# Linear attention and two gated feed-forward layers in one launch: free order of the products, new planner costs and due times, and k^T v in column halves

## Chip, cores and metric

The kernel runs on one NeuronCore of one Trainium2 chip, as one launch. The metric is the device time in microseconds of an execution. Times before and after come from several runs; one more execution of the kernel was taken with the hardware profiler, and all rows below come from it.

## What is computed

q, k and v have the shape (4, 8, 576, 64): batches, heads, tokens, width. The matrices of the two feed-forward layers have 512 x 1536 and 1536 x 512 elements and reach the kernel as 64-bit floats; q, k and v as 32-bit floats.

```python
q_s = softmax(q, axis=-1); k_s = softmax(k, axis=2)      # sums + 1e-9
kv = einsum('bhsd,bhse->bhde', k_s, v)
x = einsum('bhsd,bhde->bhse', q_s, kv)                   # -> (2304 tokens, 512)
x = (silu(x @ w_gate) * (x @ w_val)) @ w_out             # layer 0
out = ((x @ w_a) * (x @ w_b)) @ w_out2                   # layer 1
```

## The kernel before

**Stages.** The attention is done in 16 units, one for each batch b (4) and pair of heads g (4), by `attend` (L528 to L811). Each unit turns the maximum of k over the tokens (L669, L674), subtracts it and takes the exponential (L706, L710), multiplies k^T v on TensorE (L732, L733: four tiles of 128 tokens and one of the 64 last tokens of both heads), scales the two 64 x 64 blocks on the diagonal (L744, L748), normalises and turns q (L767 or L771, L780, L783) and multiplies it by the scaled blocks (L793, L803). For b = 0 q is taken less its row maximum on GpSimd (L698, L702), one ACT instruction of 1280 elements takes the exponentials of k and q (L706), a DVE reduction sums the rows (L756) and GpSimd multiplies by the reciprocals (L767). For b > 0 each row group has an exponential of its own on ACT, with the maximum as bias and the sum as a second output (L717), and GpSimd normalises (L771, L774).

The feed-forward layers work in fp32: each operand is split into two fp32r parts (high and low), and each product is three matmuls of 512 columns (high x low, low x high, high x high). A cast on ACT makes the high part (L333 or L438), and a subtraction on DVE or GpSimd makes the low one (L326). The 12 column tiles f of layer 0's matrices (`w0_0` to `w0_11`) are loaded and converted from 64 bits by `convert` (L359 to L443): absolute value (ACT L412 or DVE L414), scaling of the low word (ACT L417), clamp (DVE L419), shift (DVE L422), sign (DVE L428), the sum of the words (DVE or GpSimd L433), then the split. The activations of token block 0, `xhl0_0`, come straight from the units of b = 0.

Layer 0 runs over the blocks i = 0 and 1 (512 tokens each) tile by tile: `up` (L859, `ups` L844 for the first tile) makes the two products u of tile f, `gated` makes silu(u0) x u1 and splits it (`h`), and `down` (L886) adds the output product of the tile before, `acc`. The other stretches, layer 0's blocks 2 and 3 with the 256 last tokens, and layer 1, are three super-steps of six steps each (`step`, L1056 onwards): products p of sums and differences of blocks (L1138, seven where plain blocks would take eight), q of the last tokens (L1222), and output products o (L1248, L1250, L1257), which DVE adds into `sums` (`plus`, L1143).

**What sets the order.** `Plan` (L33 to L241) records every operation with an engine, a cost, its dependences, sometimes a second engine that may take it, and a due time, and then simulates the engines: at each moment the ready operation that is due first is issued on its engine, and this order is the program's order. `prepare` works the due times out backwards from the products' own, which `product` (L828) sets: the sum of the costs so far. `product` also adds an order edge to the product before, so all products of the feed-forward layers stand on TensorE in the order in which the code makes them, and only the attention's matmuls slip between them. `search` (L217) tries 160 sets of due times, each with some 3% of them moved by up to 3 us at random, and keeps the one with the shortest planned length.

TensorE, DVE, ACT and GpSimd each work their list strictly in that order; loads and stores stand on SP's queue, a few on ACT's.

Of the kernel before, what the change touches and what calls it, by code (L numbers as in the profile page):

```python
# [31 lines left out]
class Plan:  # L32
# [58 lines left out]
    def hop(self, first, then, other):  # L91

        if first != then:
            return other
        return 0.0 if first == "tensor" else self.SAME

    def prepare(self):
# [7 lines left out]
        for n in reversed(range(len(ops))):  # L105
# [4 lines left out]
            for s in self.succ[n]:  # L110
                if n in ops[s]["hold"]:
                    continue
                hop = self.hop(op["engine"], ops[s]["engine"], self.SLACK) + lands if n in ops[s]["deps"] else 0.0
                t = min(t, self.due[s] - hop)
# [5 lines left out]
    def order(self):  # L120
# [37 lines left out]
        while len(done) < len(ops):  # L158
# [25 lines left out]
            if port:  # L184
                port_free = t + cost
# [8 lines left out]
            free[engine] = t + cost  # L194
# [13 lines left out]
            for s in succ[n]:  # L208
                left[s] -= 1
                if not left[s]:  # L210
                    at = ops[s]["engine"]
                    is_ready(s, max([end[d] + self.hop(ops[d]["runs"][run[d]][0], at, self.HOP)
# [4 lines left out]
    def search(self):  # L217

        self.prepare()
        rng, best = random.Random(0), None  # L220
        for n in range(self.ROUNDS):
            kept = self.due
            if best:
                self.due = [d + rng.uniform(-3, 3) if rng.random() < 0.03 else d for d in kept]
            try:
                found = self.order()
            except RuntimeError:
                self.due = kept
                continue
            if best and self.length > best[0]:  # L230
                self.due = kept
            else:
                best = self.length, found
        return best[1]

    def emit(self):
        done, run, slot = self.search()
# [7 lines left out]
def kernel(  # L245
# [90 lines left out]
    def dma(fn, nbytes, reads, writes, due=None, after=(), issue=0.475, queue="sync", hold=()):  # L336
# [5 lines left out]
    def load(fn, nbytes, writes, issue=0.475):  # L342
# [4 lines left out]

    mats = [[m.bitcast(U32) for m in ms] for ms in ((w_gate, w_val, w_out), (w_a, w_b, w_out2))]
# [4 lines left out]
    TOP = 122880.0  # L353
    LEAST = 2.0 ** -15
# [102 lines left out]
    def convert_late(f, m):  # L457
# [23 lines left out]
        dma(get, P * 2 * WH * 8, [], [LOW, HIGH], issue=0.95 if m < 2 else 0.475, after=first)  # L481
# [46 lines left out]
    def attend(b, g, xhl, due):  # L528
# [63 lines left out]
        def qraw():  # L592
            return col(Q, q0, n)
# [781 lines left out]
```

## Time and profile before

| | us |
|---|---|
| median of 3 runs | 942.72 (940.71 to 944.29) |
| the profiled execution | 941.4 |
| its span, from the first to the last instruction | 939.2 |
| TensorE (PE) busy | 904.6, 4400 matmul passes |
| weight loads (PEld) busy | 753.0, beside the matmuls |
| VectorE (DVE) busy | 638.1 |
| ScalarE (ACT) busy | 518.3 |
| GpSimd (POOL) busy | 334.9 |
| mean granted TensorE clock | 0.996 of 2.4 GHz |

An engine that is busy for nearly the whole span sets the time; what another engine does counts only where the first one waits for it. A 32-bit matmul is recorded as two passes, an fp32r matmul as one. "Idle before" is the time in which an engine had nothing running before an instruction, and the name behind the arrow is what ended it.

### The profile page before, as it was taken

Reading aid. Unit: us, or ns where it says so; the run is one execution under the profiler, and the core shown is the slowest. Engines: PE = TensorE matmul, PEld = TensorE weight load, DVE = VectorE, ACT = ScalarE, POOL = GpSimd, SP = SyncE. Lnnn points to the kernel's source line nnn. Section 1 sums busy time; section 2 is a strip of 40 time slices with the busy share of each in tenths; the row PEclk is TensorE's granted clock in tenths of the full one; section 3 lists DMA queues with packets and bytes.
Section 4 is the critical chain, followed back from the end, with each engine's and each line's share of the span. In section 5 each row is a group of like instructions: output and inputs, shape, how many; then the busy total and the mean of one; then the engine's idle time right before and its main releaser. Section 6 shows DMA issues by size and latency. Waiting matters only on the chain.

```text
span 939.2 us, 12787 instructions
## 1 busy us (share of the span) xinstructions
PE 904.6 (96%) x4400; PEld 753.0 (80%) x4400; DVE 638.1 (68%) x1025; ACT 518.3 (55%) x1020; POOL 334.9 (36%) x323
## 2 busy tenths in 40 slices
PE   5599999999999999999999999999999999999998
PEld 3477777788887888888888888888888888888886
DVE  6999996544376887877778665875796444564444
ACT  4798876878675665455464546443644453333310
POOL 6534221212052322435555633442565113242210
PEclk9989999999999999999999999999999999999999
DMA  9858765464327555354322753422223210110003
GB/s 271 273 204 263 237 224 192 122 195 131 88 90 234 157 147 156 120 165 154 112 91 72 228 183 101 135 89 90 68 66 115 79 46 22 45 46 23 23 1 112
DMA packets 108153, 121.42 MB, mean 129 GB/s; under 512 B 31929, under 2 KB 83897, under 8 KB 107961
## 3 DMA queue, kind: packets, MB, share of 16 engines
q1 hardware_dynamic: 102424, 116.55, 39.7%
q10 hardware_dynamic: 5664, 4.07, 1.4%
q8 instruction: 34, 0.56, 0.2%
q14 instruction: 31, 0.25, 0.1%
HBM read 88.60 MB, written 31.98 MB: 128 GB/s over the span
## 4 chain that ended last, share of the span: by engine, by line
PE 83%; DVE 5%; ACT 4%; DMA 3%; issue 2%; SPq 1%; POOL 1%; ACTq 0%; DVEq 0%; POOLq 0%
PE p L1138 35%; PE o L1248 15%; PE u L859 10%; PE q L1222 7%; PE o L1250 6%; PE acc L886 5%; PE o L1257 2%; DMA wr<-in_moe_w_out_dram 1%; PE xt L793 1%; DVE l2w L326 1%; ACT ut L717 1%; ACT a L412 1%; PE kv L732 1%; SPq L620 1%; DMA wf<-latewr 1%
## 5 line engine op out<-in xcount | busy, mean ns | idle before, releaser
L1138 PE MATMUL p<-l2w,l2w 128*128 128x512 f32 x1512 | 352.8, 389 | 1.2 <-DVE temps L326 1.2
L1138 PEld LDWEIGHTS p<-l2w,l2w 128*128 128x128 f32 x1512 | 283.1, 188 | 61.2 <-DVE temps L326 2.5
L859 PE MATMUL u<-xhl,w 128*128 128x512 f32 x552 | 143.3, 407 | 5.0 <-DVE w L326 4.8
L326 POOL TENSOR_TENSOR l2w<-raww,l2w 128x512 fp32r<-128x512 f32 x68 | 97.2, 1434 | 94.1 <-ACT l2w L333 94.0
L333 ACT CAST l2w<-raww 128x512 fp32r<-128x512 f32 x144 | 87.9, 621 | 74.9 <-PE p L1138 39.7
L859 PEld LDWEIGHTS u<-xhl,w 128*128 128x128 f32 x552 | 101.9, 191 | 31.8 <-DVE w L326 7.1
L326 DVE TENSOR_TENSOR sums<-o,sums 128x512 f32<-128x512 f32 x120 | 82.3, 689 | 53.2 <-PE o L1248 39.4
L326 DVE TENSOR_TENSOR temps<-p,temps 128x512 f32<-128x512 f32 x90 | 62.1, 690 | 67.1 <-PE p L1138 65.9
L1248 PE MATMUL o<-l2w,hp 128*128 128x512 f32 x288 | 97.0, 391 | 0.6 <-DVE sums L326 0.6
L1150 ACT COPY temps<-p 128x512 f32<-128x512 f32 x72 | 42.4, 588 | 67.3 <-PE p L1138 67.1
L326 DVE TENSOR_TENSOR l2w<-raww,l2w 128x512 fp32r<-128x512 f32 x76 | 57.1, 762 | 26.5 <-ACT l2w L333 26.3
L886 PE MATMUL acc<-h,w 128*128 128x512 f32 x288 | 72.1, 395 | 0.0
L1222 PE MATMUL q<-rest,l2w 128*128 128x256 f32 x432 | 65.4, 283 | 0.0
L1248 PE MATMUL o<-l2w 128*128 128x512 f32 x192 | 64.4, 389 | 0.0
L1248 PEld LDWEIGHTS o<-l2w,hp 128*128 128x128 f32 x288 | 53.4, 188 | 12.6 <-DVE sums L326 1.9
L886 PEld LDWEIGHTS acc<-h,w 128*128 128x128 f32 x288 | 52.9, 188 | 10.6
L1222 PEld LDWEIGHTS q<-rest,l2w 128*128 128x128 f32 x432 | 58.6, 192 | 0.9
L1250 PE MATMUL o<-hp,l2w 128*128 128x512 f32 x144 | 48.6, 391 | 1.4 <-DVE sums L326 1.4
L1248 PE MATMUL o<-l2w,l2w 128*128 128x512 f32 x168 | 49.6, 389 | 0.0
L1250 PE MATMUL o<-l2w 128*128 128x512 f32 x144 | 48.3, 389 | 0.0
L498 POOL TENSOR_TENSOR latewr<-latewr 128x512 uint32<-128x512 uint32 x17 | 24.0, 1413 | 61.5 <-DVE latewr L493 52.7
L326 POOL TENSOR_TENSOR raww<-raww,spare 128x512 f32<-128x512 f32 x15 | 20.1, 1341 | 68.7 <-DVE l2w L326 63.2
(197 smaller groups left out, 1470.9 us busy)
## 6 DMA issues: line engine op xcount, KB each, us to landing
raww<-wf SPq DMA_DIRECT2D x36, 512.0 KB, 4.3
raww<-wf SPq DMA_DIRECT2D x36, 256.0 KB, 3.4
wf<-latewr SPq DMA_DIRECT2D x36, 256.0 KB, 3.2
wf<-a SPq DMA_DIRECT2D x16, 384.0 KB, 2.7
latewr<-in_moe_w_a_dram SPq DMA_DIRECT2D x24, 256.0 KB, 2.9
latewr<-in_moe_w_b_dram SPq DMA_DIRECT2D x24, 256.0 KB, 3.7
latewr<-in_moe_w_out_dram SPq DMA_DIRECT2D x12, 512.0 KB, 5.0
wr<-in_moe_w_gate_dram SPq DMA_DIRECT2D x22, 256.0 KB, 2.9
```

What stands on the lines that cost most here:

```text
L326: engine.tensor_tensor(out=out(), in0=x(), in1=y(), op=op)
L333: add("scalar", act_us(n), lambda: nc.scalar.copy(out=hi(), in_=src()), src_keys, [hi_key])
L412: add("scalar", act_us(e) + 0.08, lambda rows=rows, halves=halves: nc.scalar.activation(out=a(halves).bitcast(F32), in_=rows()[..., 1].bit ...
L498: engine.tensor_tensor(out=u32(), in0=u32(), in1=r()[..., 0], op=ALU.add)
L859: nc.tensor.matmul(ps()[:, 0:n], lhsT=wv[:, c, :], rhs=x()[:, xs, c, 0:n], start=(a == 0 and c == 0), stop=(a == 2 and c == KD - 1))
L886: nc.tensor.matmul(ps()[:, 0:n], lhsT=w()[:, 4 + ws, o * P:(o + 1) * P], rhs=h()[:, hs, 0:n], start=begin, stop=end)
L1138: nc.tensor.matmul(ps()[:, 0:width], lhsT=wv(o)[:, m, ws, c, :], rhs=ops_x[o][xs][1]().rearrange("p (c n) -> p c n", c=2)[:, c, 0:width], ...
L1150: add("scalar", act_us(n), lambda: nc.scalar.copy(out=to[1]()[:, 0:n], in_=ps()[:, 0:n]), [ps], [to[0]], due=main["at"] + main["soon"])
L1222: nc.tensor.matmul(ps[m]()[:, 0:256], lhsT=wv(o)[:, m, ws, c % 2, :], rhs=rest_x[xs][1]().rearrange("p (c n) -> p c n", c=KD)[:, c, :], st ...
L1248: nc.tensor.matmul(ps(), lhsT=lhs(i, hs), rhs=outs_w[i][1]()[:, ws * 512:(ws + 1) * 512], **ends)
L1250: nc.tensor.matmul(ps()[:, 0:width], lhsT=outs_w[i][1]()[:, ws * 512 + r * P:ws * 512 + (r + 1) * P], rhs=hs2[i][t][1]()[:, hs * 512:hs * ...
L1257: nc.tensor.matmul(ps()[:, o * 256:(o + 1) * 256], lhsT=outs_w[i][1]()[:, ws * 512 + at:ws * 512 + at + P], rhs=rest_h[1]()[:, (2 * i + hs ...
```

## The change

Five things are edited. `product` no longer ties a product to the one before, so the planner may issue any product whose operands are there. The planner's constants for hops between engines, DMA and issue costs are new, with new terms for the overlap of consecutive instructions of an engine (`OVER`) and of the port that DVE and GpSimd share (`PORT`); some operations have new costs. The random search is gone: the due times of 332 operations are moved by the amounts of a table, `MOVES`, and the order is made once. The units 1 and 3 of b = 0 (`BYROW`) take q's exponentials row by row on ACT as the later batches do, and for b = 0's other two units ACT may normalise q in place of GpSimd (ten `scalar.mul` of 64 columns). k^T v is computed in column halves: for each of the five token tiles two matmuls, one for each head, with 64 columns of weights and 65 moving columns (64 of v and the ones), written to the lower and upper half of the partitions; before, it was one matmul with 128 columns of weights and 130 moving ones, half of whose result was not used. `FLAT` and `NORM` are empty and change nothing.

```diff
-    SAME, HOP = 0.1, 0.17
+    SAME, HOP, TO_TENSOR, TO_GPSIMD, FROM_TENSOR = 0.033, 0.06, 0.055, 0.1, 0.2
+    OVER = dict(vector=0.08, scalar=0.115, gpsimd=0.045)
+    PORT = 0.08
-    DMA_START, DMA_END, DMA_RATE, DMA_LANES = 1.1, 1.5, 290e3, 8
-    TABLE = 1.3
+    DMA_START, DMA_END, DMA_RATE, DMA_LANES = 1.0, 1.35, 393e3, 8
+    TABLE = 1.43
-    ROUNDS = 160
+    MOVES = (
+        6, 46.2, 8, 113.4, 9, 15.3, 27, 8.1, 35, 6.2, 38, -3.9, 41, -42.6, 51, 1.8, 55, -14.4, 60, -15.5,
...
+    )
...
-                port_free = t + cost
+                port_free = t + cost - self.PORT
...
-            free[engine] = t + cost
+            free[engine] = t + cost - self.OVER.get(engine, 0.0)
...
-    def search(self):
...
+    def emit(self):
         self.prepare()
...
+        for n, us in zip(self.MOVES[::2], self.MOVES[1::2]):
+            self.due[n] += us
+        done, run, slot = self.order()
...
+    NORM = ()
+    BYROW = (1,3)
+    FLAT = ()
+    KV = 0.94
...
+        rows = b > 0 or g in BYROW
+        flat = b > 0 or g in FLAT
...
-        pk, ks = psum([P, HG, D1], "kv"), small([P, 2, HG], "ks")
+        pk, ks = psum([P, D1], "kv"), small([P, 2], "ks")
 
         def kv():
-            for r in range(R):
-                nc.tensor.matmul(pk(), lhsT=kx()[:, r, :], rhs=vx()[:, :, r, :], start=(r == 0), stop=False)
-            nc.tensor.matmul(pk(), lhsT=kl(), rhs=vg()[:, G:G + 1, :].to_broadcast([P, HG, D1]),
-                             start=False, stop=True)
-
-        add("tensor", 1.3, kv, [K_, KL, *VS, VL, (C, "ones")], [pk])
+            for r in range(R + 1):
+                for h in range(HG):
+                    lhs, rhs = (kx()[:, r, rest_cols(h)], vx()[:, h, r, :]) if r < R else (kl()[:, rest_cols(h)], vg()[:, G, :])
+                    nc.tensor.matmul(pk()[rest(h), :], lhsT=lhs, rhs=rhs, start=r == 0, stop=r == R,
+                                     tile_position=(0, h * D))
+
+        add("tensor", KV, kv, [K_, KL, *VS, VL, (C, "ones")], [pk])
...
-        if b == 0:
+        if not rows:
             add("gpsimd", pool_us(n, BROADCAST), lambda: nc.gpsimd.tensor_tensor(
                 out=qg(), in0=qg(), in1=st()[:, 3, :].unsqueeze(2).to_broadcast([P, GX, D]), op=ALU.mult),
-                [*QS, st], QS)
+                [*QS, st], QS, other=("scalar", GX * (act_us(D) - 0.115) + 0.115, lambda: [nc.scalar.mul(
+                    out=qg()[:, x], in_=qg()[:, x], mul=st()[:, 3, x:x + 1]) for x in range(GX)], False))
...
     def product(cost, fn, reads, writes, after=()):
-        n = add("tensor", cost, fn, reads, writes, due=main["at"], after=(*main["last"], *after))
+        n = add("tensor", cost, fn, reads, writes, due=main["at"], after=after)
```

The edits move work at many places. The first is GpSimd's list in the start, from the subtraction of k's maximum for unit 2 (`ut2`) to the low parts of the first weight tile (`w0_0`; `a0_0_0` and `a0_0_1` are its gate and value matrices while they are converted, `st` the maxima, sums and reciprocals of q's rows). Before, twelve rows:

```order
L767 TENSOR_TENSOR ut0_92<-ut0_92,st0_132 128x640
L687 MEMSET ut2_103 128x128
L767 TENSOR_TENSOR ut1_98<-ut1_98,st1_142 128x640
L698 TENSOR_TENSOR ut2_103<-ut2_103,st2_221 128x512
L698 TENSOR_TENSOR ut3_106<-ut3_106,st3_244 128x512
L702 TENSOR_TENSOR ut2_103<-rests_94,st2_221 128x128
L702 TENSOR_TENSOR ut3_106<-rests_94,st3_244 128x128
L687 MEMSET ut3_106 128x128
L433 TENSOR_TENSOR a0_0_0_176<-a0_0_0_176,wr0_0_0_118 128x512
L767 TENSOR_TENSOR ut2_103<-ut2_103,st2_221 128x640
L767 TENSOR_TENSOR ut3_106<-ut3_106,st3_244 128x640
L326 TENSOR_TENSOR w0_0_332<-a0_0_0_176,w0_0_332 128x512
```

And now, twelve rows from the same place:

```order
L731 TENSOR_TENSOR ut2_103<-ut2_103,st2_223 128x512
L735 TENSOR_TENSOR ut2_103<-rests_94,st2_223 128x128
L806 TENSOR_TENSOR ut1_98<-ut1_98,st1_140 128x512
L812 TENSOR_TENSOR ut1_98<-ut1_98,st1_140 128x128
L353 TENSOR_TENSOR ut3_105<-rests_94,kb3_280 128x128
L353 TENSOR_TENSOR w0_0_284<-a0_0_0_176,w0_0_284 128x512
L720 MEMSET ut3_105 128x128
L353 TENSOR_TENSOR w0_0_284<-a0_0_1_252,w0_0_284 128x512
L812 TENSOR_TENSOR ut3_105<-ut3_105,st3_310 128x128
L682 MEMSET ut4_420 64x64 x4
L685 MEMSET ut4_420 128x9
L806 TENSOR_TENSOR ut3_105<-ut3_105,st3_310 128x512
```

The two normalisations of 640 columns of units 0 and 2 are gone to ACT, those of units 1 and 3 have become pieces of 512 and 128, unit 3's q is no longer taken less its maximum here, and the sums of the words of `a0_0_0` and `a0_0_1` are gone to DVE.

The second is ACT's list up to the last of the four high parts of `xhl0_0`, which `xt3`, the output of unit 3, feeds. Before:

```order
L438 CAST w0_0_332<-a0_0_0_176 128x512
L417 ACTIVATE wr0_1_202<-wr0_1_202 128x1536
L787 COPY ut2_103<-qt2_344 128x512
L789 COPY ut2_103<-ql2_351 128x64
L789 COPY ut3_106<-ql3_357 128x64
L787 COPY ut3_106<-qt3_359 128x512
L809 DMA x0_4_374<-xq0_316 128x64
L333 CAST xhl0_0_302<-xt2_368 128x512
L333 CAST xhl0_0_302<-xt3_381 128x512
L438 CAST w0_0_332<-a0_0_1_224 128x512
L417 ACTIVATE wr0_2_259<-wr0_2_259 128x1536
```

And now:

```order
L845 COPY xq2_425<-xl2_411 128x64
L360 CAST xhl0_0_308<-xt2_416 128x512
L827 COPY ut3_105<-ql3_423 128x64
L825 COPY ut1_98<-qt1_288 128x512
L827 COPY ut1_98<-ql1_318 128x64
L448 ACTIVATE wr0_2_274<-wr0_2_274 128x1536
L360 CAST xhl0_0_308<-xt1_442 128x512
L443 ACTIVATE a0_0_2_456<-wr0_0_2_212 128x512
L847 DMA x0_4_465<-xq0_361 128x64
L825 COPY ut3_105<-qt3_459 128x512
L448 ACTIVATE wr0_3_356<-wr0_3_356 128x1536
L360 CAST xhl0_0_308<-xt3_471 128x512
```

The casts of `xt1`, `xt2` and `xt3` stand further down and apart: the rows of unit 3's exponentials (`ut3,st3`, eight of 64 and one of 128 columns), the ten normalising rows of unit 2 and three scalings of whole weight tiles now stand ahead of the last one.

The third is TensorE's list in the second super-step, where the first output product of step 6 (`o6_0`) stands. Before:

```order
L1138 MATMUL p7_1_1_5034<-l2w2_2030,l2w7_2568 128x512 x2
L1138 MATMUL p7_1_1_5034<-l2w3_2611,l2w7_2568 128x512 x2
L1138 MATMUL p7_1_1_5034<-l2w2_2030,l2w7_2568 128x512 x2
L1138 MATMUL p7_1_0_5018<-l2w4_2595,l2w8_2630 128x512 x6
L1138 MATMUL p7_1_1_5034<-l2w4_2595,l2w8_2630 128x512 x2
L1138 MATMUL p7_1_1_5034<-l2w5_2616,l2w8_2630 128x512 x2
L1138 MATMUL p7_1_1_5034<-l2w4_2595,l2w8_2630 128x512 x2
L1248 MATMUL o6_0_5089<-l2w9_2688,hp0_2900 128x512 x2
L1248 MATMUL o6_0_5089<-l2w10_2922 128x512 x2
L1248 MATMUL o6_0_5089<-l2w9_2688,hp0_2900 128x512
L1248 MATMUL o6_0_5089<-l2w10_2922 128x512
L1138 MATMUL p7_1_1_5034<-l2w5_2616,l2w9_2688 128x512 x6
```

And now:

```order
L1286 MATMUL o6_5_5311<-l2w10_3066 128x512
L1176 MATMUL p7_0_0_5103<-l2w4_2637,l2w8_2758 128x512 x6
L1176 MATMUL p8_0_0_5327<-l2w2_2169,l2w7_2702 128x512 x6
L1176 MATMUL p8_0_2_5338<-l2w3_2684,l2w7_2702 128x512 x6
L1176 MATMUL p8_0_1_5346<-l2w2_2169,l2w7_2702 128x512 x2
L1176 MATMUL p8_0_1_5346<-l2w3_2684,l2w7_2702 128x512 x2
L1176 MATMUL p8_0_1_5346<-l2w2_2169,l2w7_2702 128x512 x2
L1286 MATMUL o6_0_5360<-l2w9_2804,hp0_3057 128x512 x2
L1286 MATMUL o6_0_5360<-l2w10_3066 128x512 x2
L1286 MATMUL o6_0_5360<-l2w9_2804,hp0_3057 128x512
L1286 MATMUL o6_0_5360<-l2w10_3066 128x512
L1176 MATMUL p8_0_0_5327<-l2w4_2637,l2w8_2758 128x512 x6
```

Before, `o6_0` was the first output product of its step and stood among the products p of step 7. Now it is the last one, behind `o6_5`, and stands among the first products of step 8, while a part of step 7's `p7_0_0` has slipped behind `o6_5` too. In nine of the 18 steps (1, 4, 5, 6, 9, 10, 11, 13 and 14) the last output product now stands behind the first product p of the second step after; before, none did. Over the whole program 1062 DVE instructions stand where 1025 stood, 940 against 912 on ACT and 290 against 323 on GpSimd, DMA issues not counted.

## Rows read from the trace of the kernel before

**Rows 1.** Busy time by stage: PE, PEld, DVE, ACT, POOL; then granted clock, DMA share, GB/s.

```profile
0.00:30.00 30.00, 16.38 (x85) 12.46 (x86) 21.20 (x55) 16.07 (x31) 20.52 (x35) 1.00 0.97 297
30.00:47.20 17.20, 9.44 (x42) 6.34 (x41) 15.99 (x20) 12.57 (x17) 8.35 (x14) 0.93 0.75 230
47.20:91.10 43.90, 41.79 (x190) 33.90 (x190) 41.61 (x59) 39.18 (x87) 16.79 (x21) 0.95 0.71 232
91.10:151.90 60.80, 57.73 (x265) 45.91 (x265) 57.79 (x90) 48.50 (x90) 13.31 (x16) 1.00 0.71 231
...
286.90:934.60 647.70, 644.50 (x3169) 544.72 (x3167) 428.18 (x646) 303.91 (x541) 243.06 (x171) 1.00 0.33 103
44.95:51.77 6.82, 5.02 (x12) 3.79 (x13) 6.82 (x10) 6.43 (x19) 3.42 (x8) 0.50 1.03 341
```

**Rows 2.** Waits of PE, in total: who waited for whom; us, times, longest.

```profile
PE kx L669 <- DVE tm L326: 9.2, 4, 4.1
PE u L859 <- DVE w L326: 4.8, 4, 2.0
...
PE o L1250 <- DVE sums L326: 1.4, 2, 1.2
PE p L1138 <- DVE temps L326: 1.2, 2, 0.8
```

**Rows 3.** Chain of waits, around the last tiles of block 0: start, us, what.

```profile
128.32 2.72 PE acc L886 x12
...
150.98 0.88 DVE w L326
151.90 1.20 PE u L859 x4
```

**Rows 4.** DVE groups by shape, 0 to 151.9: count | busy us, mean ns | idle.

```profile
L326 DVE TENSOR_TENSOR w<-a,w 128x768 fp32r<-128x768 f32 x11 | 10.8, 983 | 0.0
...
L756 DVE TENSOR_REDUCE st<-ut 128x10 f32<-128x640 f32 x4 | 3.2, 811 | 1.6 <-ACT ut L706 1.6
...
L761 DVE TENSOR_SCALAR st<-st 128x9 f32<-128x9 f32 x4 | 3.0, 740 | 0.6 <-ACT ut L717 0.6
```

**Rows 5.** Single DVE instructions of the last of these shapes: start, us, what.

```profile
53.28 0.16 DVE L761 TENSOR_SCALAR st<-st 128x9 f32<-128x9 f32 x1
...
71.83 1.57 DVE L761 TENSOR_SCALAR st<-st 128x9 f32<-128x9 f32 x1 [0.24 <-ACT ut L717]
```

**Rows 6.** GpSimd in the timeline, beside the second of them.

```profile
71.20 2.08 POOL L326 TENSOR_TENSOR w<-a,w 128x768 fp32r<-128x768 f32 x1 [2.31 <-ACT w L438]
```

**Rows 7.** A GpSimd group, 0 to 47.2.

```profile
L767 POOL TENSOR_TENSOR ut<-ut,st 128x640 f32<-128x640 f32 x4 | 5.0, 1262 | 0.8 <-DVE st L764 0.8
```

**Rows 8.** ACT groups by shape, 0 to 60.

```profile
L706 ACT ACTIVATE ut<-ut 128x1280 f32<-128x1280 f32 x4 | 5.0, 1266 | 4.8 <-POOL ut L702 3.8 <-POOL ut L326 1.1
...
L717 ACT ACTIVATE ut<-ut,st 128x64 f32<-128x64 f32 x8 | 2.7, 354 | 0.0
```

**Rows 9.** ACT in the timeline.

```profile
15.26 0.67 ACT L654 COPY ut<-rests 128x64 f32<-128x64 f32 x4
```

**Rows 10.** PE in the timeline, unit 4's k^T v and small products.

```profile
57.62 1.05 PE L732 MATMUL kv<-ut 128*128 128x130 f32 x8
...
58.73 0.60 PE L780 MATMUL qt<-ident,ut 128*128 128x128 f32 x4
...
67.33 0.33 PE L803 MATMUL xl<-ut 128*128 128x64 f32 x2
67.46 3.00 PE L886 MATMUL acc<-h,w 128*128 128x512 f32 x12
```

**Rows 11.** PE in the timeline, an output product that waits for a bank.

```profile
499.98 0.72 PE L1250 MATMUL o<-hp,l2w 128*128 128x512 f32 x2 [1.16 <-DVE sums L326]
```

**Rows 12.** The end: SP's last issues.

```profile
934.01 2.50 SPq L1294 DMA_DIRECT2D out_dram<-rs  x4
```

More of the change, by code (lines that the diff above doesn't have):

```diff
@@ L1 @@
-import random
 from contextlib import ExitStack
@@ L89, in add, with hop @@
         return n
[L91 to L95, printed above, removed]
+    def hop(self, first, then):
+        if first == "tensor":
+            return 0.0 if then == "tensor" else self.FROM_TENSOR
+        return dict(gpsimd=self.TO_GPSIMD, tensor=self.TO_TENSOR).get(then, self.SAME)
     def prepare(self):
@@ L211, in order @@
                     at = ops[s]["engine"]
-                    is_ready(s, max([end[d] + self.hop(ops[d]["runs"][run[d]][0], at, self.HOP)
+                    is_ready(s, max([end[d] + self.hop(ops[d]["runs"][run[d]][0], at)
                                      for d in ops[s]["deps"]] + [issued[d] for d in ops[s]["order"]]))
@@ L480, in convert_late @@
         A1, LOW, HIGH = [(buf, (at, x)) for x in range(3)]
-        dma(get, P * 2 * WH * 8, [], [LOW, HIGH], issue=0.95 if m < 2 else 0.475, after=first)
+        dma(get, P * 2 * WH * 8, [], [LOW, HIGH], issue=0.95 if m < 2 else 0.37, after=first)
         add("scalar", act_us(2 * WH) + 0.08, lambda: nc.scalar.activation(
@@ L523, in load_rests @@
                 in_=src[b, :, SM:S, :].rearrange("(g h) s d -> h s g d", h=HG)[h]),
-                SL * KD * D * 8, [], [(rests, (at, h))], issue=0.65, queue="scalar")
+                SL * KD * D * 11.4, [], [(rests, (at, h))], issue=0.65, queue="scalar")
     AT_BANKS = [("at0", "at1", "gv0", "gv1"), *[("at0", "at1")] * 3]
@@ L615, in load_rest @@
                 load(lambda h=h: nc.sync.dma_start(
-                    out=dst()[rest(h), rest_cols(h)], in_=src[b, g * HG + h, SM:S, :]), SL * D * 8, [keys[h]])
+                    out=dst()[rest(h), rest_cols(h)], in_=src[b, g * HG + h, SM:S, :]), SL * D * 18, [keys[h]], issue=0.56)
         def load_v():
@@ L621, in load_v @@
                     out=vx()[:, h, :, 0:D], in_=v[b, g * HG + h, 0:SM, :].rearrange("(p r) d -> p r d", r=R)),
-                    P * R * D * 5, [(C, f"v{h}")])
+                    P * R * D * 6.6, [(C, f"v{h}")], issue=0.67)
         def qrl():
@@ L643, in attend @@
             load_v()
-            load(lambda: nc.sync.dma_start(out=vg()[:, G, 0:D], in_=v[b, hs, SM:S, :]), P * D * 8, [VL])
+            load(lambda: nc.sync.dma_start(out=vg()[:, G, 0:D], in_=v[b, hs, SM:S, :]), P * D * 12, [VL], issue=0.57)
             kr_, qr_, KR, QRL = kl, qrl, [*KLS, (A, NO)], [*QLS, (Q, "q" + NO)]
@@ L772, in attend @@
                 out=qx(), in0=qx(), in1=st()[:, 3, 0:G].rearrange("p (h r) -> p r h", h=HG).unsqueeze(3).to_broadcast(
-                    [P, R, HG, D]), op=ALU.mult), [*QS, (st, 3)], [Q_, *QS])
+                    [P, R, HG, D]), op=ALU.mult), [*QS, (st, 3)], [Q_, *QS],
+                other=("scalar", G * (act_us(D) - 0.115) + 0.115, lambda: [nc.scalar.mul(
+                    out=qx()[:, r, h], in_=qx()[:, r, h], mul=st()[:, 3, h * R + r:h * R + r + 1])
+                    for r in range(R) for h in range(HG)], False) if b in NORM else None)
             add("gpsimd", pool_us(P, BROADCAST), lambda: nc.gpsimd.tensor_tensor(
```

74 lines of the change are left out of this document (30 added, 44 removed), and 38 rows, old and new, of the table MOVES.

## The prediction

> **What bounds the kernel now.** Read the table by stage first [rows 1]. From 286.9 us to the last matmul TensorE is busy for 644.5 of 647.7 us: there it is the bound, and only its own work and some 3 us of waits can go. Up to 151.9 us it is another picture. PE is busy for 16.38 + 9.44 + 41.79 + 57.73 = 125.3 of 151.9 us, and DVE for 21.20 + 15.99 + 41.61 + 57.79 = 136.6. After 30 us DVE has 6.5 us of idle time in 122, while PE has 12.9. Next come PE's waits [rows 2]: 9.2 us for the maxima of k (`tm`), nearly all at the start and for unit 4, and 4.8 us for the low part of a weight tile (`w`), both made by DVE. The chain of waits says the same at the end of this stage [rows 3]: the low part of the last tile, `w0_11`, ends on DVE, and PE takes it at 151.90. So the stage ends when DVE has worked through the conversions, and PE has just enough to do beside them. The clock is a small term: PE idled before unit 4's maxima came, the granted clock fell to half, 1.2 GHz, from 44.95 to 51.77 us [rows 1], and PE's 5.02 busy us there would have been 2.5 at the full 2.4.
>
> The sum below is made against the profiled execution, 941.4 us, of which 2.2 lie around the span. It is 1.3 below the median of the runs, 942.7, on which the forecast is stated.
>
> **The conversions, up to `w0_11`.** What DVE has to do before this point changes little. The order gives it two more low parts of 128x768, at 0.98 us [rows 4], three sums of words of 512 columns that GpSimd had, some 0.7 us each by the same rate, and five more scalings of 64x64, small ones. It loses two row sums of 0.81 us [rows 4], and a few tiny ones. That is 2.0 + 2.1 + 1 - 1.6 - 1 = +2.5 us.
>
> GpSimd slows DVE down, and gets less to do. The same 128x9 instruction takes 0.16 us at 53.28 and 1.57 at 71.83 [rows 5], where a GpSimd subtraction ran from 71.20 to 73.28 [rows 6]. Its mean over the stage is 0.74 [rows 4], so this one form loses 4 x 0.58 = 2.3 us, and others lose less each; I estimate 10 us for all. GpSimd is busy for 20.5 + 8.4 + 16.8 + 13.3 = 59 us of the stage [rows 1]. The order takes from it the four normalisations of 640 columns, 5.0 us [rows 7], two low parts of some 2 us [rows 6], the three sums and two subtractions of 512 columns, and gives it two pieces of 512 back: about 12 us, a fifth. I take a fifth of the 10: -2 us. It could be nothing, or 4.
>
> DVE's idle time is 15.3 us: 8.8 before 30 us, most of it waiting for the first loads, which stand on SP in the same order as before, and 6.5 later. A gain there rests on what waits where. For two units of the start, unit 1 and 3, q no longer goes GpSimd, ACT (1280 columns at once, 1.27 us), DVE, GpSimd, but straight from the maximum into ACT, and DVE's row sums, before which it idled for 1.6 us [rows 4], are halved. I take that 1.6, and half of the later 6.5: -5 us. Bounds: -8 (all but most of the first 8.8) and -2.
>
> The cover is ACT. It gets sixteen exponentials of 64 columns at 0.35 [rows 8], two of 128, and twenty normalising pieces, four of which would take 0.67 by a plain copy's row [rows 9]: 5.6 + 0.8 + 3.3, less half of two 1280s of 1.27 [rows 8], is +8.4 us before `xhl0_0` is complete. Up to 47.2 us it is busy for 16.07 + 12.57 = 28.6 us [rows 1], so 37 of 47 us is still not full, but it is why I let no more than 5 us go. With it the first tile's last products come later than before, and tile 1 follows them earlier, at 44 to 46 instead of 47.2 us. PE has no say here: from 47.2 to 151.9 it is busy for 99.5 us, so it would be through by 145.
>
> Together: 2.5 - 2 - 5 = **-4.5 us**, PE takes `w0_11` at 147.4. With the planner's free order, products of other tiles fill PE's gaps in this stage, but their number is the same, so this moves idle time and doesn't end it.
>
> **k^T v in halves.** Ten passes take 58.73 - 57.62 = 1.11 us [rows 10], 16 times. Now there are 20 passes of 65 columns. No row has 64 columns of weights. The nearest with few moving columns is unit 4's last product: two passes of 64 columns take 67.46 - 67.33 = 0.13 us, 0.065 each [rows 10]. Were the halves worked one after the other, that is 1.30 us, +0.19; were two always worked at once, 0.65, -0.46. I take the middle, -0.14, since the two halves use different columns of the array but come from one list. In the stage up to 151.9 DVE hides it; the eight units of b = 2 and 3 lie where PE is the bound: **-1.1 us**. DVE's two small instructions on the sums stay two.
>
> Against this stands a rule: the Trainium skill (TensorEngine Tiling (Array Packing), Key Properties) says that a change of the tiling mode, not just of the tile, drains TensorE, and each of the 16 groups now changes it twice. What the rows would make of such an emptied array: twelve matmuls take 2.72 us from the first to the next one's start [rows 3], but 3.00 to their own end [rows 10], so 0.28 each time, 0.56 a unit, and then the units would cost PE time instead of giving any. No row of this trace has a change of mode. It is the fourth rival.
>
> **Waits later on.** PE's waits for evictions, `sums` and `temps`, come to 1.4 + 1.2 us [rows 2]; the longest, 1.16 us at 499.98 [rows 11], stood behind long DVE work. Costs nearer to the trace should put evictions ahead of it: I take **-2 us** of the 2.6. Bounds: -2.6, and a loss, the third rival.
>
> **The end.** Before, the last output is `rs1`, stored in pieces of 64 rows: SP's last four issues take 2.50 us, 0.63 each [rows 12], and two of them follow the last eviction. Now the last chunk is a `sums` with one issue: **-0.4 us**.
>
> Sum: -4.5 - 1.1 - 2 - 0.4 = -8.0. 942.7 - 8.0 = **934.7 us**.
>
> **Rivals.**
> 1. *More goes than that.* DVE loses 4 us less to GpSimd and idles 8 us less: 2.5 - 4 - 8 = -9.5; k^T v at -0.46 gives -3.7, waits -2.6, the end -0.4: -16.2, 926.5 us. For it: everything needed has a row. Against: ACT's added 8.4 us.
> 2. *DVE stays the bound.* More work (+2.5), no relief from GpSimd, idle time down by 2: +0.5, and the rest -3.5: 939.7 us, no change that can be told. For it: DVE's 6.5 idle us of 122.
> 3. *Overtaking keeps buffers.* In nine of the 18 steps the last output product now stands behind the first product of the second step after. Its operands, the split `hp` and the output weights in three ring slots, stay in use, and the casts that refill them wait on ACT, with all that is queued behind them there and on DVE; then PE runs into a bank that isn't evicted. If this costs PE one wait of the longest kind, 1.16 us [rows 11], at each of the 17 borders between steps in place of the two that it has, it is 17 x 1.16 - 2.6 = +17 where I have -2: 934.7 + 2 + 17 = 954; at two in each of the nine steps, 18 x 1.16 - 2.6 = +18: 955. It decides from twelve such waits on: 934.7 + 2 - 2.6 + 12 x 1.16 = 948, slower. Against: PE has 644.5 of 647.7 us there with the same pools, and DVE and ACT are busy for 428 and 304 of it [rows 1], so a late cast has room to catch up.
> 4. *The mode change drains PE.* 1.30 + 0.56 instead of 1.11 is +0.75 a unit, 6 us on the late eight, where I have -1.1; the early eight lie under DVE. 934.7 + 7.1 = 941.8: no change.
>
> **Chances.** Forecast 0.52 (its own range 929 to 938.5), first rival 0.20, second 0.13, third 0.07, fourth 0.08. A measurement of this kernel can tell 0.5% (4.7 us) from no change. Faster by more than that, under 938.0: nearly all of the forecast, all of the first rival, a fourth of the second: 0.50 + 0.20 + 0.04 = 0.74. Slower, over 947.4: 0.06 of the third. Same: 0.20. The range 924 to 944 leaves out the third rival, the far end of the first, and a little of the fourth: 2 in 10.
>
> **What would show it.** In the new profile: PE's first matmul on `w0_11` near 147, DVE busy near 137 us up to there and idle near 10; tile 1 at 44 to 46 us and no stretch at 1.2 GHz after it, or a short one; k^T v's span from its first pass to the next instruction near 0.97 us; PE's waits for `sums` and `temps` under 1 us; one issue after the last eviction. I am wrong if `w0_11` still comes at 151 or later (second rival), if PE waits by the step after 286.9 us (third), or if k^T v takes over 1.3 us (fourth).

## The result and the profile after

| | before | after |
|---|---|---|
| median | 943.15 us (940.71 to 944.29) | 953.75 us (951.19 to 955.30) |
| ratio | | 1.011, 95% interval 1.008 to 1.014 |
| span of the profiled execution | 939.2 us | 951.6 us |

Slower by 10.6 us, where 8 us of gain were forecast. The table by stage in the changed kernel answers to [rows 1], with the same borders:

```profile
0.00:30.00 30.00, 15.22 (x96) 9.15 (x96) 22.16 (x49) 19.43 (x67) 13.92 (x29) 1.00 0.95 286
30.00:47.20 17.20, 12.42 (x68) 8.36 (x68) 16.07 (x28) 17.20 (x48) 6.26 (x14) 1.00 0.85 276
47.20:91.10 43.90, 39.03 (x179) 30.00 (x179) 41.53 (x57) 39.19 (x72) 17.19 (x19) 0.96 0.68 223
91.10:151.90 60.80, 58.98 (x314) 46.16 (x314) 57.01 (x95) 49.10 (x90) 12.12 (x16) 1.00 0.71 226
151.90:286.90 135.00, 131.59 (x721) 101.57 (x721) 77.37 (x172) 95.53 (x254) 26.79 (x63) 1.00 0.48 143
286.90:948.00 661.10, 652.33 (x3187) 548.49 (x3185) 451.69 (x664) 298.46 (x538) 216.62 (x150) 1.00 0.31 98
```

Up to 151.9 us nothing is won: PE is busy for 125.7 us (125.3 before) and DVE for 136.8 (136.6). From 151.9 to 286.9 PE now idles for 3.4 us instead of 0.3; this is the row before:

```profile
151.90:286.90 135.00, 134.74 (x655) 109.71 (x656) 72.64 (x160) 98.11 (x257) 32.89 (x67) 1.00 0.43 129
```

After 286.9 it idles from row to row up to its last matmul, at 947.9: 947.9 - 286.9 - 652.3 = 8.7 us instead of 3.2. PE is also busy 5.0 us longer in all (909.6 against 904.6), and the end is 0.9 us shorter (3.8 us from PE's last matmul to the end of the span, before 4.6). Sum: idle time -0.3 + 3.1 + 5.5, busy time +5.0, the end -0.9, together the +12.4 of the span.

The waits of PE in the changed kernel (who waited for whom; us in total, times, longest), over the whole span, against [rows 2]:

```profile
PE kx L702 <- DVE tm L353: 8.5, 4, 4.2
PE u L897 <- ACT s L908: 4.0, 2, 3.6
...
PE p L1176 <- DVE temps L353: 3.4, 3, 1.5
...
PE p L1176 <- ACT temps L1188: 1.8, 1, 1.8
PE o L1288 <- DVE sums L353: 1.7, 2, 1.5
...
PE o L1286 <- DVE sums L353: 0.8, 1, 0.8
...
PE u L897 <- DVE w L353: 0.7, 1, 0.7
```

The waits for weight tiles (`w`) have nearly gone, 4.8 to 0.7 us, and waits for ACT's silu (`s`) stand in their place. The waits for evictions (`sums`, `temps`), which were to vanish, grew from 3.2 to 7.7 us. What stands in front of one of them is seen in the timeline (start, us, what; behind the arrow, what ended the idle time):

```profile
493.98 0.43 DVE L515 TENSOR_SCALAR latewr<-latewr 128x512 uint32<-128x512 uint32 x1 [0.79 <-DMA latewr<-in_moe_w_out_dram]
...
494.36 2.39 POOL L353 TENSOR_TENSOR l2w<-r,l2w 128x1024 fp32r<-128x1024 f32 x1 [4.86 <-ACT l2w L360]
494.44 2.59 DVE L519 TENSOR_SCALAR latewr<-latewr 128x512 f32<-128x512 f32 x1
...
496.95 0.68 DVE L353 TENSOR_TENSOR temps<-p,temps 128x512 f32<-128x512 f32 x1
...
497.69 0.50 PE L1176 MATMUL p<-l2w,l2w 128*128 128x512 f32 x1 [1.20 <-DVE temps L353]
```

DVE stands still until a late weight has landed, then begins its clamp just when GpSimd works, and the clamp takes 2.59 us, where the median of all 36 such clamps is 0.43. Only then does DVE empty the bank that PE waits for. Such idle time of ACT and DVE for loads, from 287 us on, grew more than sixfold. After, the largest of ACT's and DVE's waits that a DMA ended:

```profile
ACT latewr L517 <- DMA latewr<-in_moe_w_out_dram: 12.1, 7, 3.8
ACT latewr L517 <- DMA latewr<-in_moe_w_b_dram: 6.0, 5, 3.7
ACT latewr L517 <- DMA latewr<-in_moe_w_a_dram: 5.7, 4, 2.9
...
DVE latewr L515 <- DMA wf<-latewr: 10.1, 7, 4.0
```

And the largest in the kernel before:

```profile
ACT l2w L333 <- DMA raww<-wf: 2.7, 2, 2.4
...
DVE ob L902 <- DMA x<-ob: 1.4, 1, 1.4
```

All such rows come to 55 us after and 8.6 us before. They are called loads below, but some are not: `wf<-latewr` is the store of a converted weight, which has to land before its buffer is written again.

### The profile page after: what moved, and what is told of

The parts are those of the page before. It is cut to its first block, busy times and chain, and to the rows that moved or that the text cites. A ratio compares the mean times of both kernels' runs of the same rounds, so it can differ in the third digit from the quotient of the medians.

```text
span 951.6 us, 13107 instructions
## 1 busy us (share of the span) xinstructions
PE 909.6 (96%) x4560; PEld 743.7 (78%) x4560; DVE 666.4 (70%) x1062; ACT 518.9 (55%) x1066; POOL 292.9 (31%) x290
## 4 chain that ended last, share of the span: by engine, by line
PE 49%; DVE 8%; DMA 4%; issue 1%; ACT 1%; POOL 1%; SPq 0%; DVEq 0%; ACTq 0%; POOLq 0%
PE p L1176 25%; PE o L1286 15%; PE q L1260 5%; PE o L1288 3%; DMA latewr<-in_moe_w_out_dram 2%; DVE l2w L353 2%; DVE temps L353 1%; PE o L1295 1%; DVE sums L353 1%; DMA wf<-latewr 1%; POOL latewr L529 1%; DVE latewr L519 1%; DVE latewr L524 1%; DMA latewr<-in_moe_w_b_dram 1%; DVE raww L353 0%
## 5 line engine op out<-in xcount | busy, mean ns | idle before, releaser
L1176 PE MATMUL p<-l2w,l2w 128*128 128x512 f32 x1512 | 359.9, 391 | 5.4 <-DVE temps L353 3.4
L353 POOL TENSOR_TENSOR l2w<-raww,l2w 128x512 fp32r<-128x512 f32 x64 | 91.4, 1430 | 210.0 <-ACT l2w L360 203.3
L924 PE MATMUL acc<-h,w 128*128 128x512 f32 x288 | 78.5, 404 | 0.4 <-DVE h L353 0.3
L353 DVE TENSOR_TENSOR l2w<-raww,l2w 128x512 fp32r<-128x512 f32 x80 | 63.0, 796 | 17.8 <-ACT l2w L360 16.5
L924 PEld LDWEIGHTS acc<-h,w 128*128 128x128 f32 x288 | 52.2, 189 | 13.3 <-DVE h L353 1.5
L1286 PEld LDWEIGHTS o<-l2w 128*128 128x128 f32 x192 | 36.0, 188 | 7.6
```

The source lines that it names most:

```text
L353: engine.tensor_tensor(out=out(), in0=x(), in1=y(), op=op)
L924: nc.tensor.matmul(ps()[:, 0:n], lhsT=w()[:, 4 + ws, o * P:(o + 1) * P], rhs=h()[:, hs, 0:n], start=begin, stop=end)
L1176: nc.tensor.matmul(ps()[:, 0:width], lhsT=wv(o)[:, m, ws, c, :], rhs=ops_x[o][xs][1]().rearrange("p (c n) -> p c n", c=2)[:, c, 0:width], ...
L1286: nc.tensor.matmul(ps(), lhsT=lhs(i, hs), rhs=outs_w[i][1]()[:, ws * 512:(ws + 1) * 512], **ends)
```

## Experiments

**Theories.** *Theory 1*: the planner's new constants may be nearer to the trace, but a plan made with them leaves no slack, so that whatever comes late stops an engine that works its list in order. *Theory 2*: overtaking keeps buffers and banks (the prediction's third rival). *Theory 3*: the table of moved due times. All kernels were timed beside the kernel before. The kernels named `b_` start from the kernel before and, but for the three of k^T v in halves, let the random search choose their order anew; how much the time scatters among orders of the search that are planned equally long was not tried. In the table, "idle" is PE's idle time from 286.9 to 930 us, "loads" the idle time of ACT and DVE after 287 us that a DMA ended.

| kernel | median, us | ratio to before | idle | loads |
|---|---|---|---|---|
| before | 943 | | 3.2 | 8.6 |
| changed | 953.75 | 1.008 to 1.014 | 8.7 | 55 |
| b_free | 949.59 | 1.005 to 1.009 | 2.5 | 8 |
| a_chain | 968.18 | 1.023 to 1.028 | 13.8 | 59 |
| a_nomoves | 967.54 | 1.023 to 1.029 | 13.3 | 69 |
| b_const | 973.44 | 1.031 to 1.034 | 13.5 | 71 |
| b_over | 955.91 | 1.012 to 1.015 | 5.7 | 32 |
| b_hop | 948.82 | 1.005 to 1.007 | 3.8 | 19 |
| b_const_place | 975.35 | 1.032 to 1.037 | 15.6 | 49 |
| b_const_margin | 978.06 | 1.033 to 1.039 | 17.3 | 66 |
| a_oldconst_nomoves | 960.68 | 1.016 to 1.021 | 1.5 | 15 |
| b_dma | 956.27 | 1.011 to 1.018 | 5.7 | 49 |
| b_nodma | 951.70 | 1.006 to 1.012 | 3.1 | 34 |
| b_const_safe | 957.28 | 1.013 to 1.018 | 2.0 | 7 |
| a_safe | 965.69 | 1.021 to 1.027 | 1.5 | 5 |
| a_safe_nomoves | 960.87 | 1.015 to 1.022 | 6.5 | 10 |
| b_byrow | 944.26 | 1.001 to 1.004 | 3.9 | 17 |

### Overtaking and the table

`b_free` drops the chain in the kernel before:

```diff
-        n = add("tensor", cost, fn, reads, writes, due=main["at"], after=(*main["last"], *after))
+        n = add("tensor", cost, fn, reads, writes, due=main["at"], after=after)
```

> The kernel before with one edit: products are no longer chained, so they may overtake each other; costs, constants and the random search stay. Theory 1 (the new constants leave the engines' lists without slack; overtaking is harmless): within 3 us of before. Theory 2 (overtaking keeps buffers and banks, the third rival): +6 to +12 us, with new waits of PE for evictions after 287 us. Theory 3 (the table of moved due times is at fault): within 3 us of before.

Measured: +7 us, but none of it where theory 2 puts it: after 286.9 us PE idles less than before (2.5 us). The new waits lie at 150 to 178 us, at the border to the units of b = 2, where PE waits 1.7 us for `w` and 2.5 for `km`. The larger part of the loss is not in waits at all: PE is busy for 910.2 us instead of 904.6, and up to 286.9 us its mean granted clock is 0.97 instead of 0.99.

`a_chain` is the reverse edit in the changed kernel, and `a_nomoves` sets `MOVES = ()`.

> The changed kernel with the products chained again; constants, table of moved due times, k^T v in halves and the units by rows stay. Theory 1 (constants without slack): still +6 to +12 us against before, with waits of PE for evictions of 3 us or more after 287 us. Theory 2 (overtaking keeps buffers): within 3 us of before, or faster by the 2 us of k^T v. Theory 3 (the table): still +6 to +12.

> The changed kernel with an empty table, so no due time is moved; free order, constants, halves and units by rows stay. Theory 1 (constants without slack): still +5 to +15 us against before. Theory 2 (overtaking): still +6 to +12, since the products still overtake. Theory 3 (the table is at fault): within 3 us of before or faster.

Measured: +25.7 and +25.0 us, more than any theory expected. Taking away either one costs the changed kernel some 14 us, so neither alone makes its loss: theories 2 and 3, which expected a time within 3 us of before, fall. Something else costs more than the change's loss. (`a_chain` is no clean reversal, since the table's amounts were found for the free order.)

### The constants

`b_const` puts all new constants into the kernel before; `b_over` and `b_hop` one group each:

```diff
+    OVER = dict(vector=0.08, scalar=0.115, gpsimd=0.045)
+    PORT = 0.08
...
-                port_free = t + cost
+                port_free = t + cost - self.PORT
...
-            free[engine] = t + cost
+            free[engine] = t + cost - self.OVER.get(engine, 0.0)
```

```diff
-    SAME, HOP = 0.1, 0.17
+    SAME, HOP, TO_TENSOR, TO_GPSIMD, FROM_TENSOR = 0.033, 0.06, 0.055, 0.1, 0.2
...
```

> The kernel before with the new constants of the planner alone (hops, overlap, port, DMA, table load); chain, random search, operations and k^T v as before. Theory 1 (constants without slack are at fault): slower by 10 to 25 us, PE's waits after 287 us at 5 us or more instead of 3.4. Theory 2 (the free order is at fault in the changed kernel): within 4 us of before.

> The kernel before with one group of the new constants: the overlap of consecutive instructions on DVE, ACT and GpSimd, and of the port. If theory 1 holds and the overlap makes the loss (DVE's list planned about 80 us shorter): at least half of what all constants cost, +5 us or more. If the hops do it: within 3 us of before.

> The kernel before with the other group: the hops between engines (0.033 to 0.2 in place of 0.1 and 0.17). If theory 1 holds and short hops make the loss: +5 us or more. If the overlap does it: within 3 us of before.

Measured: +30, +12.5 and +5.5 us. The constants alone make the kernel before slower by three times the change's loss, and by more than the 10 to 25 us expected. In the profiled execution the loss of `b_const` has three like parts: PE idles 10.7 us longer up to 286.9 us, 10.3 us longer behind it, and is busy 10.6 us longer. Two ways in which they could do so were tried next: `b_const_place` keeps each operation on the engine that it has before, and `b_const_margin` plans 0.5 us between an operand and TensorE, and between a buffer's last use and its next (the diff is against `b_const`):

```diff
-    SAME, HOP, TO_TENSOR, TO_GPSIMD, FROM_TENSOR = 0.033, 0.06, 0.055, 0.1, 0.2
+    SAME, HOP, TO_TENSOR, TO_GPSIMD, FROM_TENSOR = 0.033, 0.5, 0.5, 0.1, 0.2
```

> The kernel before with the new constants, but each of the 555 operations that two engines may take stays on the engine that it has before (a table of letters). All constants alone cost +30 us. If the loss comes from work that the new constants move from GpSimd to DVE: within 10 us of before. If it comes from the order on each engine, planned without slack: still +20 us or more.

> The kernel before with the new constants, but with 0.5 us in the plan between an operand's end and TensorE, and between a buffer's last use and its next (0.055 and 0.06 in the new constants, 0.17 before). If the loss of +30 us comes from a plan that sends work to PE the moment that it expects the operand: at most +18 us. If it comes from the durations (overlap, DMA) alone: +22 us or more.

Measured: +32 and +35 us, the second branch of either expectation. Neither work that went from GpSimd to DVE nor a lack of room just ahead of PE is the cause. `a_oldconst_nomoves` gives the changed kernel the old constants and no table:

> The changed kernel with the constants of before (hops, no overlap, no port term, DMA, table load) and without the table, whose amounts were found for the others; free order, units by rows, k^T v in halves and the operations' new costs stay. If the constants make the loss: -3 to +8 us against before (the free order alone cost +7). If the units by rows or the new costs of operations make it: +15 us or more.

Measured: +18 us, which is the second expectation: by the time alone the constants would be cleared. But after 286.9 us PE idles for only 1.5 us, so there the loss is gone; nearly all of it lies ahead of that, which is taken up below.

### Loads

Theory 1 was split for the next runs. *Theory 1a*: the constants for loads do it, by listing work ahead of the landing that it needs. *Theory 1b*: the overlap does it, by planning DVE's and ACT's lists too densely. `b_dma` has the third group alone, `b_nodma` the other two, and `b_const_safe` all, but with loads that are planned to land later (the diff is against `b_const`):

```diff
-    DMA_START, DMA_END, DMA_RATE, DMA_LANES = 1.0, 1.35, 393e3, 8
+    DMA_START, DMA_END, DMA_RATE, DMA_LANES = 1.1, 3.0, 290e3, 8
```

> The kernel before with the third group of the new constants: loads planned to start and land sooner and at 393 instead of 290 KB a us (and the table load's cost). In the trace with all new constants ACT and DVE wait for loads after 287 us for 71 us, where before they wait for 9. Theory 1a (casts and conversions are listed before their loads land, and evictions stand behind them): +6 to +15 us, with 25 us or more of such waits. Theory 1b (the overlap term does it, by listing all of DVE's and ACT's work too densely): within 4 us of before.

> The kernel before with the new hops and the overlap and port terms, but the old constants for loads and tables. All together cost +30 us, hops alone +5.5, overlap alone +12.5. Theory 1a (loads): +18 us at most, under 40 us of waits for loads on ACT and DVE after 287 us. Theory 1b (overlap): +18 us or more, whatever the waits for loads.

> All new constants, but loads planned to land 1.5 us later than with the old ones. Theory 1a (loads): at most +10 us against before, and waits for loads on ACT and DVE after 287 us back to about 10 us. Theory 1b (overlap): still +15 us or more, though those waits are gone.

Measured: +13.5, +9 and +14.5 us. The first two are as theory 1a has it. The third is not: 1a expected at most +10, and the time is near the +15 of 1b. It missed by the stretch ahead of 287 us; behind it, the waits for loads are gone as 1a expected. The rows by stage of `b_const`:

```profile
0.00:286.90 286.90, 249.40 (x1157) 194.08 (x1158) 198.07 (x370) 201.03 (x462) 78.78 (x143) 0.98 0.60 187
...
286.90:930.00 643.10, 629.63 (x3064) 527.30 (x3063) 435.79 (x654) 303.34 (x541) 220.30 (x153) 1.00 0.33 101
```

And of `b_const_safe`:

```profile
0.00:286.90 286.90, 250.16 (x1156) 197.93 (x1157) 198.74 (x379) 200.15 (x456) 73.14 (x141) 0.96 0.60 186
...
286.90:930.00 643.10, 641.10 (x3135) 541.67 (x3134) 440.76 (x671) 311.45 (x555) 199.30 (x144) 1.00 0.33 102
```

The early row hardly moves. In the late one PE's idle time goes from 13.5 to 2.0 us, with the overlap and the hops as they were, and the waits for loads from 71 to 7. The constants for loads alone are not enough for the whole of it, since `b_dma` idles for only 5.7 us there and `b_nodma` for 3.1: it takes both groups to come to 13.5. The last two runs ask the same of the changed kernel, with its table and without:

> The changed kernel with one edit: loads are planned to land later (start 1.1, end 3.0, 290 KB a us); the table and all else stay. If loads that land after their plan make the changed kernel's late waits: ACT and DVE wait for loads after 287 us for at most 15 us (55 in the changed kernel), PE idles there for at most 4 us (8.7), and the stretch after 287 us is 4 to 7 us shorter. The start may shift either way, since the table's amounts were found for another order. If the late waits come from the free order or the table: PE still idles 7 us or more there.

> The same without the table. The changed kernel without the table alone is +25 us against before, with 69 us of waits for loads and 13.3 us of PE's idle time after 287 us. If the loads make these: at most 15 us of such waits, at most 4 us of idle time, and 10 to 15 us faster than that, +10 to +15 against before, the rest from the stretch before 287 us. If not: still +20 us or more.

```profile
286.90:930.00 643.10, 641.59 (x3136) 541.72 (x3136) 443.60 (x673) 308.56 (x551) 207.55 (x146) 1.00 0.32 102
```

That is `a_safe`: 1.5 us of idle time instead of 8.7, and 5 us of waits for loads instead of 55. So the late waits of the changed kernel come from when loads are planned to land; the free order and the table are still in `a_safe`. Its whole time is worse all the same, 965.7 us: PE's work up to 286.9 falls from 257.2 to 243.1 us. The table's amounts belong to another order: with the new constants it adds 2.6 us of work by then (`a_nomoves` has 254.7), with the later landing it takes 7.9 away (`a_safe_nomoves` has 250.9). `a_safe_nomoves` came to +18 where +10 to +15 was expected, with 6.5 us of idle time instead of 13.3, more than the 4 that were expected.

Over the whole table, the seven kernels that plan loads with the new constants wait for them for 49 to 71 us and PE idles for 5.7 to 17.3 us late; the ten that plan them as before or later wait for 5 to 34 us and PE idles for 1.5 to 6.5.

### Units by rows

`b_byrow` puts `rows = b > 0 or g in (1, 3)` and ACT's normalisation into the kernel before.

> The kernel before with units 1 and 3 of b = 0 by rows and q's normalisation open to ACT, as in the changed kernel; constants, chain, search and k^T v as before. The prediction took 5 us of DVE's idle time and 2 us of GpSimd's drag from this: the last weight tile's low part 4 us earlier and -4.5 us against before. Rival, ACT's added 8 us take the cover away or the order shifts with it: 0 to +6 us, and the last low part at 151 us or later.

Measured: +1.5 us (1.001 to 1.004). The rival is right: in the order that the search then chose, the units by rows bring nothing. The last low part ends at 153.07 us instead of 151.84, and DVE idles for 18.9 us up to 151.9 instead of 15.3.

### k^T v in halves

Three kernels with before's order word for word: `b_kv` has the halves in all 16 units, `b_kv_late` in those of b > 0, `b_kv_late2` in those of b > 1.

```diff
+         half = b > 1
...
+             if half:
+                 for r in range(R + 1):
+                     for h in range(HG):
...
+                         nc.tensor.matmul(pk()[rest(h), :], lhsT=lhs, rhs=rhs, start=r == 0, stop=r == R,
+                                          tile_position=(0, h * D))
+                 return
```

> The kernel before, its order word for word, with k^T v in column halves alone. From the changed kernel's trace a unit takes 0.80 us instead of 1.11. If only PE's time where PE is the bound counts: eight late units x 0.31 = -2.5 us against before, the early eight hidden under DVE. If a changed tiling mode costs PE time that the trace shows at other instructions: 0 or slower, up to +6. If TensorE's time counts everywhere: -5 us.

> The kernel before, its order word for word, with k^T v in column halves for b > 0 alone; the four units of b = 0 keep the whole width. Clock theory (with all 16 units in halves TensorE did less in the first 47 us, the granted clock stood at half for longer there, 20.5 us against 6.8, and the gain went back): no more stretches at half clock than before, and the gain of the late units shows: -2.5 us against before, 8 x 0.31. Rival, the changed tiling mode costs at the neighbouring instructions what the unit saves: 0 again, as with all 16.

> The kernel before, its order word for word, with k^T v in column halves for b = 2 and 3 alone, where PE is the bound. With the halves in b > 0 a unit and its two neighbours took 1.39 us where they took 1.57 before, so -0.19 a unit, and the loss lay between 47 and 155 us. If that is right, -1.5 us against before (8 x 0.19), with the start as before. If the neighbours lose as much as the unit gains elsewhere: 0.

Measured: 942.88 against 942.52 (ratio 0.999 to 1.001), 943.79 against 943.34 (0.999 to 1.002), and 940.74 against 942.89 (0.996 to 0.999): the last one is faster than both kernels of this study. PE's timeline around the same unit, before and then in `b_kv_late2`:

```profile
245.71 2.20 PE L886 MATMUL acc<-h,w 128*128 128x512 f32 x9
247.75 1.05 PE L732 MATMUL kv<-uc,ua 128*128 128x130 f32 x8
...
248.78 0.94 PE L886 MATMUL acc<-h,w 128*128 128x512 f32 x3
249.56 0.60 PE L780 MATMUL qt<-ident,ua 128*128 128x128 f32 x4
```

```profile
246.62 2.20 PE L894 MATMUL acc<-h,w 128*128 128x512 f32 x9
248.75 0.80 PE L736 MATMUL kv<-uc,ua 128*64 128x65 f32 x20
249.48 0.96 PE L894 MATMUL acc<-h,w 128*128 128x512 f32 x3
250.28 0.60 PE L788 MATMUL qt<-ident,ua 128*128 128x128 f32 x4
```

From the first pass to what follows, k^T v goes from 1.03 to 0.73 us. But the nine matmuls ahead of it take 2.13 instead of 2.04 and the three behind it 0.80 instead of 0.78, so from first row to last it is 3.85 to 3.66: -0.19 a unit, -1.5 us for eight. The other seven late units show the same 0.73.

In `b_kv` the first 155 us eat that up. In its profiled execution the granted clock stands at half there four times, where before it did once, from 44.95 to 51.77 us [rows 1]:

```profile
27.17:34.00 6.83, 5.75 (x19) 4.42 (x20) 4.76 (x13) 3.67 (x7) 4.94 (x4) 0.50 1.04 365
37.41:40.82 3.41, 3.41 (x9) 2.63 (x10) 3.31 (x4) 2.46 (x4) 2.74 (x5) 0.50 0.09 21
47.65:54.48 6.83, 5.39 (x13) 4.23 (x14) 6.83 (x8) 6.81 (x21) 2.66 (x6) 0.50 1.03 338
105.68:109.09 3.41, 3.41 (x8) 2.76 (x9) 2.88 (x6) 3.41 (x15) 0.00 (x0) 0.50 0.84 253
```

PE takes the last weight tile's low part at 154.94 instead of 151.90 [rows 3], 3.0 us late, and the late units give half of it back (its last matmul ends 1.6 us later than before's). Over the whole span the mean clock was 0.988 to 0.993 in the 11 runs of `b_kv` and 0.990 to 0.996 in the 15 of before beside them, so the profiled one, with 0.988, is at the low end. `b_kv_late` has before's stretch at 45 us, yet two more at 61.5 and 105.9 us, behind waits of PE of 1.5 and 2.3 us, where its expectation had no more stretches than before; `b_kv_late2` has only the one that before has. So the halves pay where PE is the bound, and ahead of it waits came, and stretches at half clock behind them, that used up the gain. That the fewer passes cause the stretches was not tried apart, and in the changed kernel's own order the halves were not taken out.

## Why the prediction was wrong

The forecast took 8.0 us off; the span of the profiled execution grew by 12.4. The 20.4 us between them are the waits later on (7.5), PE's busy time with k^T v (6.1), the conversions (4.2) and the stretch from 151.9 to 286.9 us (3.1), less 0.5 at the end.

- **"Waits later on", -2 us: the step that failed.** It said: costs nearer to the trace should put evictions ahead. PE's waits for evictions grew instead from 3.2 us (2.6 in the forecast, which left out 0.6) to 7.7 and its whole late idle time by 5.5 us, and `a_safe`, with loads planned to land later, takes all of that back. For loads the new costs are not nearer to the trace. The new constants plan a load of 512 KB at 1.0 + 524288 / 393000 + 1.35 = 3.7 us, the old ones at 1.1 + 1.8 + 1.5 = 4.4. The trace's median from issue to landing for `raww` of 512 KB is 4.7 us after and 4.3 before. For `latewr` of 512 KB, which the longest waits are for, it is 4.4 us after. So the old constants were about right for the middle load, and under them, in the order of before, ACT and DVE waited 8.6 us for loads; under the new ones they reach scalings and absolute values before the weights are there, with the evictions queued behind. The Trainium skill (DMA: Bandwidth & Descriptors, Anatomy of one DMA) fits 2.0 us plus the bytes at 436 GB/s, for GpSimd's own path, which would be an estimated 3.2 us here; the traces show more, and they decide.
- **From 151.9 to 286.9 us**, +3.1 us, which no term foresaw: in DVE's waits, those for k's loads of the units of b = 2 and 3 (`tm`) come to 7.9 us, where before they were 1.4:

```profile
DVE tm L353 <- DMA uc<-in_k_dram: 7.9, 6, 2.7
```

```profile
DVE tm L326 <- DMA uc<-in_k_dram: 1.4, 2, 1.2
```

  That looks like the late waits, but it is not shown to be the cause: in `a_safe` they are 2.3 us, and PE idles there for 9.1 us. `b_free`, which has the free order and the old constants, has 5.1 us of them and 4.4 us of PE's idle time, so the free order is the nearer suspect. The cause stays open.
- **The conversions, -4.5 us: the second step that failed; 0.3 us came.** In the changed kernel's timeline PE's first matmuls on tile 1, and on DVE the last two low parts:

```profile
49.48 4.61 PE L897 MATMUL u<-xhl,w 128*128 128x512 f32 x12 [3.62 <-ACT s L908]
```

```profile
149.67 1.82 DVE L353 TENSOR_TENSOR w<-a,w 128x768 fp32r<-128x768 f32 x2
```

  The last one ends at 151.49 us (151.84 before). DVE had the forecast amount of work, 136.8 us against "near 137", but its idle time stayed at 15 where it was to fall to 10. The forecast took 5 us of idle time from the units by rows, and `b_byrow` shows none of it. The wait of 1.6 us that they were to remove is gone, but DVE now waits elsewhere: 2.1 us for loads of q, 1.7 for k^T v, 1.5 for ACT's absolute values, 1.2 for a weight. ACT, the cover that the forecast named, was as full as it said, 36.6 of 47.2 us against "37 of 47", and yet too full for the first tile: tile 1 starts at 49.48 us, behind 3.6 us of waiting for ACT's silu, not at 44 to 46, and 3.4 us at 1.2 GHz follow from 49.7. The second rival had named this stage rightly.
- **k^T v, -1.1 us: right sign, other parts.** Eight late units gave -1.5 by the rows. Two halves do run at once: in `b_kv_late2` the two passes of a pair start 0.007 us apart, and 20 passes start within 0.58 us, 0.031 each, less than the prediction's bound of 0.65 us. The fourth rival's mechanism is there too, but small: the neighbours lose 0.09 and 0.02 us, and k^T v's last pass holds up its successor for 0.15 us instead of 0.03. That is 0.23 us a unit and not the 0.56 of the estimate. The Trainium skill (TensorEngine Tiling (Array Packing), Key Properties) says that a change of the tiling mode drains TensorE, and the rows above agree. The early eight, costed at nothing, cost some 2 us by the medians of `b_kv` and `b_kv_late2`, in the order of before.
- **The end, -0.4 us:** 0.9 us shorter, more than forecast.
- **The third rival, 954 us, hit the number by luck.** PE does run into banks that aren't evicted, but for 7.7 us in all, where the rival had 20, and `b_free`, which has the overtaking alone, has fewer such waits than before after 287 us, 1.3 us instead of 3.2.
- **PE's added 5.0 busy us** were not forecast. By the starts of all its passes k^T v takes 5.8 us less, and the products acc 4.1, p 3.2 and the turns of q 2.0 us more, in pauses too short to be listed as waits and, for p, in 3.4 us at half clock behind the 1.8 us wait at 712 us.

Open stays what the start loses: `b_const_safe` and `a_oldconst_nomoves` are still 15 and 18 us slower than before, nearly all of it ahead of 287 us. The rows show where it goes. Up to 286.9 us PE idles for 36.7 and 40.1 us instead of 26.8, and the mean granted clock is 0.96 and 0.93 instead of 0.99. Before, and then `a_oldconst_nomoves`:

```profile
0.00:286.90 286.90, 260.08 (x1233) 208.32 (x1234) 209.24 (x379) 214.43 (x479) 91.87 (x152) 0.99 0.61 190
```

```profile
0.00:286.90 286.90, 246.83 (x1294) 189.09 (x1295) 197.12 (x362) 210.94 (x506) 91.66 (x149) 0.93 0.60 186
```

What sets off these waits is not shown. For `a_oldconst_nomoves` the free order (+7), the units by rows (+1.5) and the early halves (some 2) do not sum to 18, and the new costs of single operations were not tried alone. Nor did any run make the changed kernel faster: its late waits are explained, its 10.6 us as a whole are not.

## What to carry to other kernels

A planner that orders in-order queues must not underrate what others wait for, here the landing of loads: an operation listed ahead of its landing stops all that stands behind it. So compare such constants with the times from issue to landing in the trace, lean to the long side, and look at the off-path engines' waits for DMA, not only at PE's. It is no cure for all: the later landing took `b_const` from +30 to +14.5 us, and the changed kernel, whose table was found for another plan, from +10.6 to +23. An edit that saves passes should be tried by stage: the same halves won 2 us where PE was the bound, and with the early units added the gain was gone.

## What the runs showed of the hardware

Matmuls with 64 columns of weights on two halves of the array run at once, though they stand one behind the other in one list: in `b_kv_late2` 0.031 us a pass of 65 moving columns, where [rows 10] has 0.065 for one of 64 at full width. Going over and back costs 0.23 us in all. And with less work for a PE that idles anyway the rest can become slower: in `b_kv`'s profiled execution 18.0 us of PE's busy time passed at 1.2 GHz up to 110 us, where it had been 5.0 before. That the one brings the other was not tried apart.
